# Attention scores in plain fp32 on 64 rows a head, both heads of a pair together, in a kernel whose order is planned

## The chip, the cores and the metric

The kernel runs on one core of one Trainium2 chip. The metric is the device time of one execution in microseconds (us), lower is better. A core has a matrix engine (PE in the profile, its weight loads PEld), a vector engine (DVE), an activation engine (ACT), a general engine (POOL), and queues that start transfers (SP and ACT here). Matmuls write to PSUM, a small memory of banks; the rest works in on-chip SBUF.

## The reference, cut to what matters

```python
B, H, S, D = 4, 8, 576, 64
scores = scale * q @ k.T                 # per batch and head: 576 x 64 times 64 x 576
scores += bias(pos)                      # a small network on relative positions, same for all batches
attn = exp(scores - max); attn /= sum
x = (attn @ v)                           # heads side by side: B x 576 x 512
h = gelu(x @ w_in); u, v = halves(h)     # 512 -> 1024
x = x + (u * (w_sg @ norm(v) + b_sg)) @ w_out
theta = x @ w_theta                      # second block
u = x + w_tok_r @ (x cos theta) + w_tok_i @ (x sin theta)
out = u + relu(u @ w_ch)
```

## The kernel before, in words

The program has four stretches. First the position bias of all heads is built (tiles `mk`, `pb`, `bt`, `cc`, `bias`). Then comes attention, four batches of four **pairs** of heads, with the first half of the MLP of batches 0 to 2 and the reading of its weights (`rawwi`, `cvawi`, `wi`, `ws`) woven between. Then the second half of the MLP (`op`) with the reading of the later weights (`wo`, `wt`, `wk`), and last the second block (`tp`, `yp`, `cp`).

A head has 576 query rows: four tiles of 128 (`t` = 0 to 3) and a remainder of 64. The remainders of the two heads of a pair share one tile (kind 2), so a pair has nine tiles. For each tile: the scores are made by PE into a PSUM tile `s` of two banks (two halves of 288 keys); DVE adds the bias and takes the extreme of each row (`e`, `m`); ACT takes the exponential with its row sums (`e`, `sums`), ACT copies it to 16 bits (`p`) and POOL subtracts to get the low part; a DMA transpose on SP's queue turns `p` into `pT`; PE multiplies by `v` into `px` (14 matmuls). There are two `s` tiles, so one can be filled while the other is read. At the end of a head (`group_end`) DVE divides `px` by the sums into `xf` and splits it into `x16` (shown as `x`), and after the ninth tile one DMA transpose makes `xp` of the pair, which goes to memory as `dx`.

PE takes the scores in the reduced format `float32r`. To keep precision `prep` splits, for each head, k into a high and a low part (`kh`, `kl`) and q likewise. Queries stand in `qs` with the high part on partitions 0 to 63 and the low part on 64 to 127; k is held twice, on both halves. So each score half is two matmuls over all 128 rows: `kh` and `kl` against `qs`. `prep` runs once a head: loads `raw` (k twice and v) and `rq` (q), copies `kh` and `qs`, subtractions `kl` and `qs`, and v in two 16-bit parts (`v`).

What runs in which order is decided when the program is built. Every operation is recorded; a planner (`Rec.plan`) plays through a model of the engines and always issues, per engine, the ready operation with the smallest key. The key is a due time in the code plus a number per tile name from the table `SHIFT`; where an operation may go to one of several engines, the table `BIAS` weighs the choice. Each engine then executes its list strictly in that order. All work is emitted from one line (L366 before), so the profile is read by tile names.

Of the kernel before, what the change touches and what calls it, by code (L numbers as in the profile page):

```python
# [218 lines left out]
}  # L219
SHIFT = {  # L220
    "aw": -17.4929, "bias": 41.9326, "biasr": -68.9186, "bsg": 97.9286, "bt": -5.7555, "c": -279.9533, "ca": 22.1144,
    "cc": 295.8081, "ch": -73.6056, "ci": 36.2217, "cl": 17.4554, "cp": 15.2786, "cvaw_ch": 69.6045,
    "cvaw_out": -194.7794, "cvaw_theta": 8.5825, "cvaw_tok": -207.7246, "cvawi": -0.5182, "cvsw_ch": 161.0008,
    "cvsw_out": 0.6877, "cvsw_theta": -99.9127, "cvsw_tok": 85.3798, "cvswi": 2.3671, "ds": 47.8704, "e": -0.6132,
    "eps": 169.8, "fa_c": -50.561, "fa_v": 185.4902, "fa_wi": -255.4938, "fa_ws": 58.9062, "fb_c": -277.5272,
    "fb_v": 19.4726, "fb_wi": -86.0368, "fb_ws": 64.453, "fc_c": 164.9752, "fc_v": 223.2589, "fc_wi": 7.0491,
    "fc_ws": 28.1163, "fd_c": -314.7184, "fd_v": -444.6712, "fd_wi": -6.1476, "fd_ws": -20.5742, "fs_c": 244.1602,
    "fs_v": -273.363, "fs_wi": -108.0749, "fs_ws": -26.7084, "g": 98.9891, "gg": 3.2775, "ghs": -197.3784,
    "gr": 14.9268, "gsc": -167.0231, "gts": 44.5279, "gtu": -15.6392, "gtv": -6.823, "halfpi": 90.4852, "i": 26.7498,
# [3 lines left out]
    "prow": -7.3266, "ps_wi": 22.646, "ps_ws": -28.4781, "px": -152.186, "qs": -4.2259, "r": 3.9345, "raw": -5.9457,  # L233
    "raww_ch": -200.3987, "raww_out": -60.0335, "raww_theta": 85.7967, "raww_tok": 89.0463, "rawwi": -219.9835,
# [346 lines left out]
class K:  # L581
# [257 lines left out]
    def prep(self, b, h):  # L839
        nc, a = self.nc, self.p_att  # L840
        u = f"{b}_{h}"
        qs = self.qs[(b * H + h) % 3]
        raw = a.tile([P, 2, S], F32, tag="raw", bufs=1, name=f"raw{u}")
        qr = a.tile([64, S], F32, tag="rq", bufs=1, name=f"rq{u}")
        kh = a.tile([P, S], F32R, tag="kh", bufs=3, name=f"kh{u}")
        kl = a.tile([P, S], F32R, tag="kl", bufs=3, name=f"kl{u}")
# [9 lines left out]
        self.v16[h] = v16  # L856
        self.cp(v16[:, 0], vr, self.sv)
        nc.vector.scalar_tensor_tensor(v16[:, 1, 0:5], vr[:, 0:5], self.sv, v16[:, 0, 0:5],
                                       op0=ALU.mult, op1=ALU.subtract)

    def att_tile(self, b, p, kind, t, sums, px):
        nc, a = self.nc, self.p_att
        u = f"{b}_{p}_{kind}_{t}"
        ps = self.ps_s.tile([P, 2, 512], F32, tag="sc", bufs=2, name=f"s{u}")
        hd = (self.hd[2 * p], self.hd[2 * p + 1])
        if kind < 2:
            qs, kh, kl = hd[kind]
            ops = [(qs[:, 128 + t * P:128 + (t + 1) * P], m) for m in (kh, kl)]
            bias = self.bm[t][:, 2 * p + kind]
        else:  # L870
            ops = [(hd[1][0][:, 0:128], hd[1][1]), (hd[0][0][:, 64:128], hd[0][1]),
                   (hd[0][0][:, 64:128], hd[0][2]), (hd[1][0][:, 0:128], hd[1][2])]
            bias = self.bm[4][:, p]
        for i, (w, m) in enumerate(ops):
            for n in range(2):
                nc.tensor.matmul(ps[:w.shape[1], n, :SH], w, m[:, n * SH:(n + 1) * SH],
                                 start=(i == 0), stop=(i == len(ops) - 1))
# [8 lines left out]
        self.exps.append(nc.scalar.activation(s, s, AF.Exp, bias=m[:, 1:2], scale=-1.0, accum_out=sums[:, t:t + 1]))  # L886
# [454 lines left out]
```

## Time and profile before

| | before |
|---|---|
| median of 3 runs, us | 963.27 (957.67 to 965.01) |
| span of the profiled execution, us | 948.8 |
| mean granted TensorE clock | 0.881 |
| busy: PE, DVE, ACT, POOL | 736.5, 747.9, 562.5, 441.5 us |

The span runs from the first to the last instruction. The time of the profiled execution itself is not listed apart from the three runs; their median is 14.5 us over the span, which lies before the first and behind the last instruction. Engine rows give busy time and, behind the bar, the idle time just before such instructions and what ended it. Busy PE time counts the tail of a matmul too, so a full bar is not full throughput.

### The profile page before, as it was taken

How to read it: one execution, taken by the hardware profiler on the slowest of the kernel's cores; microseconds unless marked ns; L12 is line 12 of the kernel's file. 1: busy time of each engine (PE TensorE's matmuls, PEld its weight loads, DVE VectorE, ACT ScalarE, POOL GpSimd, SP SyncE). 2: the span in 40 equal slices, each digit the busy share in tenths (PEclk: the TensorE clock that was granted, in tenths of full speed). 3: DMA queues.
4: the chain of work that ended last, by engine and by line, in shares of the span. 5: the costliest groups of instructions: out<-in, count | busy, mean ns of one | idle time of the engine just before them, and what ended most of it. 6: DMA issues, size and time to landing. Idle time of an engine off the chain costs nothing.

```text
span 948.8 us, 19542 instructions
## 1 busy us (share of the span) xinstructions
PE 736.5 (78%) x7322; PEld 598.6 (63%) x7322; DVE 747.9 (79%) x1544; ACT 562.5 (59%) x1144; POOL 441.5 (47%) x373
## 2 busy tenths in 40 slices
PE   4345445665575895979878989899778999999998
PEld 3345444554464664655555655576757899999998
DVE  8798978889987788998999796898998884372622
ACT  7413148868776777877877684765555673261510
POOL 1667784545545464564556563145643532041310
PEclk9667876756669888899979999999988999999999
DMA  7300019889899999999989995645541110010001
GB/s 250 104 1 2 1 30 255 166 167 217 152 197 207 204 194 183 192 225 218 190 186 199 231 179 154 208 138 176 182 134 48 34 52 34 1 51 1 26 26 50
DMA packets 223871, 124.79 MB, mean 132 GB/s; under 512 B 195616, under 2 KB 195744, under 8 KB 223776
## 3 DMA queue, kind: packets, MB, share of 16 engines
q1 hardware_dynamic: 214560, 101.88, 50.0%
q10 hardware_dynamic: 9216, 21.67, 7.9%
q8 instruction: 57, 0.93, 0.4%
q14 instruction: 38, 0.31, 0.1%
HBM read 62.17 MB, written 14.16 MB: 80 GB/s over the span
## 4 chain that ended last, share of the span: by engine, by line
PE 38%; DVE 28%; DMA 15%; issue 10%; ACT 7%; POOL 1%; SPq 0%; ACTq 0%; DVEq 0%; POOLq 0%
PE yp L366 11%; DMA pT<-p 6%; DVE mk L366 5%; PE cp L366 4%; PE s L366 4%; DVE e L366 4%; PE op L366 3%; PE tp L366 3%; PE pb L366 3%; PE px L366 3%; DMA xp<-x 3%; PE up L366 2%; DVE x L366 2%; DVE cvaw_tok L366 2%; PE sp L366 2%
## 5 line engine op out<-in xcount | busy, mean ns | idle before, releaser
L366 POOL TENSOR_TENSOR p<-e,p 128x576 f16<-128x576 f32 x144 | 194.4, 1358 | 152.7 <-ACT p L366 132.5
L366 PE MATMUL s<-kh,qs 128*128 128x288 f32 (+1 forms) x320 | 94.0, 390 | 63.9 <-DVE m L366 39.6
L366 ACT ACTIVATE e<-e,m 128x576 f32<-128x576 f32 x144 | 110.4, 767 | 42.1 <-DVE m L366 37.7
L366 PE MATMUL px<-v,pT 128*128 128x64 f16 (+1 forms) x2240 | 102.5, 206 | 41.1 <-DMA pT<-p 34.3
L366 PEld LDWEIGHTS <-pT 128*128 128x128 f16 (+1 forms) x2240 | 89.0, 110 | 68.8 <-DMA pT<-p 46.1
L366 PE MATMUL yp<-wk,z 128*128 128x288 f32 x864 | 118.3, 296 | 0.7 <-ACT z L366 0.4
L366 PEld LDWEIGHTS yp<-wk,z 128*128 128x128 f32 x864 | 115.6, 188 | 1.8 <-ACT z L366 0.9
L366 PEld LDWEIGHTS s<-kh,qs 128*128 128x128 f32 (+1 forms) x320 | 59.3, 222 | 85.5 <-DVE m L366 31.7
L366 PE MATMUL pb<-ch,mk 128*128 128x64 f16 x720 | 60.0, 213 | 65.6 <-ACT cc L366 34.4
L366 DVE CUSTOM_DVE_ANT_0 e<-s,bias 128x576 f32<-128x576 f32 x128 | 95.7, 751 | 13.0 <-PE s L366 11.4
L366 ACT ACTIVATE p<-e 128x576 f16<-128x576 f32 x140 | 92.8, 671 | 18.3 <-DMA pT<-p 13.5
L366 PEld LDWEIGHTS <-mk 128*128 128x128 f16 x1440 | 58.4, 111 | 68.0 <-DVE mk L366 54.8
L366 PE MATMUL s<-kl,qs 128*128 128x288 f32 (+1 forms) x320 | 84.9, 362 | 6.4 <-DVE kl L366 6.1
L366 DVE TENSOR_TENSOR mk<-ds,th 128x2048 f16<-128x2048 f16 x45 | 79.5, 1817 | 5.2 <-PE pb L366 5.1
L366 POOL TENSOR_TENSOR bias<-bt,cc 128x512 f32<-128x512 f32 x36 | 62.1, 1745 | 42.8 <-ACT cc L366 24.0
L366 PE MATMUL op<-sp_g,wo 128*128 128x288 f32 x384 | 65.0, 328 | 14.6 <-DVE x L366 9.3
L366 PEld LDWEIGHTS op<-sp_g,wo 128*128 128x128 f32 x384 | 59.1, 212 | 21.3 <-DVE x L366 7.0
L366 PEld LDWEIGHTS s<-kl,qs 128*128 128x128 f32 (+1 forms) x320 | 62.1, 228 | 10.2 <-DVE kl L366 9.2
L366 ACT ACTIVATE cc<-pb,ci 128x512 f32<-128x512 f32 x45 | 29.6, 683 | 62.5 <-DVE bt L366 56.7
L366 PE MATMUL vp<-wi,xT 128*128 128x512 f16 (+1 forms) x240 | 64.2, 395 | 2.2 <-DVE gg L366 2.2
L366 PE MATMUL sp<-ws,n 128*128 128x64 f16 (+1 forms) x384 | 58.7, 293 | 2.8 <-DVE n L366 2.7
L366 DVE TENSOR_TENSOR x<-x,yp 128x576 f32<-128x576 f32 x16 | 12.1, 754 | 61.6 <-PE yp L366 61.6
(228 smaller groups left out, 1651.5 us busy)
## 6 DMA issues: line engine op xcount, KB each, us to landing
raw<-kv ACTq DMA_DIRECT2D x19, 576.0 KB, 4.9
raw<-kv SPq DMA_DIRECT2D x13, 576.0 KB, 4.7
raww_tok<-w_tok SPq DMA_DIRECT2D x18, 288.0 KB, 3.0
vr<-v_all SPq DMA_DIRECT2D x12, 384.0 KB, 3.8
xx<-dx SPq DMA_DIRECT2D x16, 288.0 KB, 3.2
out<-oo SPq DMA_DIRECT2D x16, 288.0 KB, 2.1
xT<-dx SPq DMA_DIRECT2D x7, 576.0 KB, 5.2
gr<-dg SPq DMA_DIRECT2D x14, 288.0 KB, 3.3
```

Of the source, the lines that this page charges most:

```text
L366: getattr(getattr(self.nc, name), m)(*[res(x) for x in a], **out)
```

## The change

The two heads of a pair now lie side by side: k and q of head 0 on partitions 0 to 63, of head 1 on 64 to 127, unsplit (`kq`). A score half is one plain fp32 matmul over the 64 rows of its head; the four of a tile pair are issued in the order head 0, head 1, head 0, head 1, each head into its own `s` tile. `kh`, `kl`, `qs` and `rq` are gone. `prep` runs once a pair. The main ends of both heads are one (`pair_main`, 8 columns of sums, `xf` 128x512), and the remainder tile stands at the start of the pair (`pair_rem`), but in the first pair at its end. The planner's model of a 64-row matmul is changed, and both tables and a few of its constants have new values; some loads and weights may now choose another queue or engine.

```diff
 BIAS = {
-    ("gg", "gpsimd"): -9.3524, ("gg", "vector"): -1.4198, ("kh", "scalar"): -12.8265, ("kh", "vector"): 14.8773,
+    ("bsg", "scalar"): -41.5201, ("bsg", "sync"): -39.1168, ("g", "scalar"): -6.4798, ("g", "sync"): -12.4768,
...
-        return rhs.cols * (4.0 if rhs.t.dt == F32 else 1.068 if rhs.t.dt == F32R else 1.0), rhs.shape[0] / P
+        n = rhs.cols * (4.0 if rhs.t.dt == F32 else 1.068 if rhs.t.dt == F32R else 1.0)
+        return (n / 2 if rhs.shape[0] == 64 else n), rhs.shape[0] / P
...
-        kr, vr = raw[:, 0], raw[:, 1].rearrange("p (c d) -> p c d", d=D)
-        self.cp(kh, kr)
-        self.tt(("gpsimd", "vector"), kl, kr, kh.bitcast(F32), ALU.subtract)
-        self.cp(qs[0:64, 64:640], qr)
-        self.tt(("gpsimd", "vector"), qs[64:P, 64:640], qr, qs[0:64, 64:640].bitcast(F32), ALU.subtract)
-        v16 = a.tile([P, 2, 9, D], F16, tag="v16", bufs=3, name=f"v16{u}")
+        kq = a.tile([P, 2, S], F32, tag="kq", bufs=2, name=f"kq{u}")
+        raw = a.tile([P, 2, S], F32, tag="raw", bufs=1, name=f"raw{u}")
+        for o in (self.ld(kq, self.d["kq"][b, p]), self.ld(raw, self.d["vp"][b, p])):
+            nc.dep(o, self.th)
+        v16 = a.tile([P, 2, 2, 9, D], F16, tag="v16", bufs=2, name=f"v16{u}")
...
+    def scores(self, b, p, t):
+        k, q = self.kq[:, 0], self.kq[:, 1]
+        if t < 4:
+            tiles = [self.ps_s.tile([P, 2, 512], F32, tag="sc", bufs=2, name=f"s{b}_{p}_{e}_{t}") for e in range(2)]
+            parts = [(tiles[e], slice(0, P), slice(64 * e, 64 * e + 64)) for e in range(2)]
+        else:
+            tiles = [self.ps_s.tile([P, 2, 512], F32, tag="sc", bufs=2, name=f"s{b}_{p}_2_0")]
+            parts = [(tiles[0], slice(64 * e, 64 * e + 64), slice(64 * e, 64 * e + 64)) for e in range(2)]
+        for n in range(2):
+            for ps, o, r in parts:
+                ops.append(nc.tensor.matmul(ps[o, n, :SH], q[r, t * P:min(S, t * P + P)], k[r, n * SH:(n + 1) * SH],
+                                            start=True, stop=True))
+        for o in ops:
+            for ps in tiles:
+                nc.dep(o, ps.t.first)
...
+    def pair_main(self, b, p, sums, x16):
+        r = self.inverse(sums, u)
+        xf = a.tile([P, 4, P], F32, tag="xf", bufs=1, name=f"xf{u}")
+        nc.vector.tensor_tensor(xf.rearrange("p t (e d) -> p (t e) d", e=2), self.px.rearrange("p t e d -> p (t e) d"),
+                                r.bc(2, D), op=ALU.mult)
+        self.cp(x16[:, :4, 0], xf)
+        self.tt(("gpsimd", "vector"), x16[:, :4, 1], xf, x16[:, :4, 0], ALU.subtract)
...
-        order = [(e, t) for e in range(2) for t in range(4)] if q else [(e, t) for t in range(4) for e in range(2)]
+        if q:
+            self.pair_rem(b, p, self.px[:, 3, 1], x16)
+        for t in range(4):
+            ps = self.scores(b, p, t)
+            for e in range(2):
+                self.att_tile(b, p, e, t, ps[e], sums[:, 2 * t + e:2 * t + e + 1], self.px[:, t, e])
+        self.pair_main(b, p, sums, x16)
```

PE's list before, in batch 2, second pair (`s2_1_0_1` is batch 2, pair 1, head 0, tile 1; `up` and `sp` are the MLP of batch 0):

```order
5591 L366 MATMUL sp0_0_5411<-ws_2204,n16_0_3909 128x512
5592 L366 LDWEIGHTS wi_2205
5593 L366 MATMUL up0_2_5412<-xT0_3904,wi_2205 128x512
5594 L366 MATMUL s2_1_0_0_5451<-kh2_2_5016,qs0_121 128x288 x2
5595 L366 MATMUL s2_1_0_1_5471<-kh2_2_5016,qs0_121 128x288 x2
5596 L366 LDWEIGHTS wi_2205
5597 L366 MATMUL up0_2_5412<-xT0_3904,wi_2205 128x512
```

An `s` row here stands for both key halves of one tile (x2); the `kl` part of both tiles follows some 30 rows further on. The same place in PE's list now:

```order
5721 L377 MATMUL px_2127<-v162_0_4647,pT2_0_1_1_5070 128x64
5722 L377 MATMUL s2_1_0_1_5168<-kq2_1_4702 128x288
5723 L377 MATMUL s2_1_1_1_5194<-kq2_1_4702 128x288
5724 L377 MATMUL s2_1_0_1_5168<-kq2_1_4702 128x288
5725 L377 MATMUL s2_1_1_1_5194<-kq2_1_4702 128x288
5726 L377 LDWEIGHTS n16_0_3950
5727 L377 MATMUL sp0_2_5028<-ws_2151,n16_0_3950 128x512
```

Before, two tiles of one head stand in the two `s` buffers, each begun with `kh` and finished with `kl` further on; now tile 1 of both heads fills both buffers in one group of four.

DVE's list before, around the first tile of that pair (`v16`, `kl`, `qs` are the preparation of pairs to come, `r` and `xf` the end of pair 0):

```order
655 L366 TENSOR_SCALAR v162_2_5345<-raw2_2_5360,fc_v_157 128x576
656 L366 TENSOR_TENSOR kl2_2_5046<-raw2_2_5360,kh2_2_5016 128x576
657 L366 SCALAR_TENSOR_TENSOR v162_2_5345<-raw2_2_5360,fc_v_157,v162_2_5345 128x320
658 L366 TENSOR_TENSOR qs1_120<-rq2_3_5214,qs1_120 64x576
659 L366 TENSOR_SCALAR r2_0_0_5355<-sm2_0_0_4780 128x4
660 L366 TENSOR_SCALAR r2_0_1_5384<-sm2_0_1_5103 128x4
661 L366 ISA e2_1_0_0_5462,m2_1_0_0_5400<-s2_1_0_0_5451,bias0_78 128x576
```

Four of these seven rows prepare heads of pairs to come. DVE's list now, around the second tile of that pair:

```order
587 L377 SCALAR_TENSOR_TENSOR gg0_2_5192<-sp0_2_5028,gsc_118,bsg_164 128x512
588 L377 TENSOR_TENSOR x16_2_0_5163<-xfr2_0_2_4888,x16_2_0_5163 64x128
589 L377 ISA e2_1_0_1_5227,m2_1_0_1_5141<-s2_1_0_1_5168,bias1_77 128x576
590 L377 ISA m2_1_0_1_5141 128x1
591 L377 TENSOR_SCALAR m2_1_0_1_5141<-m2_1_0_1_5141 128x1
592 L377 ISA e2_1_1_1_5274,m2_1_1_1_5165<-s2_1_1_1_5194,bias1_77 128x576
```

The `kl` and `qs` rows between the `e` rows are gone from DVE's list, and the `e` of head 0 and of head 1 of one tile number follow each other.

## Rows read from the trace of the kernel before

**Rows 1.** By stretch: length, busy PE, PEld, DVE, ACT, POOL, clock, DMA share, GB/s

```profile
0.00:131.00 131.00, 60.69 (x1422) 58.30 (x1423) 112.96 (x129) 50.62 (x91) 79.22 (x54) 0.79 0.20 65
131.00:300.00 169.00, 102.34 (x1020) 83.96 (x1016) 147.55 (x390) 127.31 (x298) 87.15 (x80) 0.68 0.91 184
300.00:425.00 125.00, 95.30 (x1042) 68.50 (x1041) 106.70 (x261) 94.55 (x193) 69.53 (x59) 0.87 1.01 198
425.00:583.00 158.00, 138.64 (x1515) 90.46 (x1514) 140.90 (x359) 120.10 (x239) 86.34 (x75) 0.97 0.98 192
583.00:734.00 151.00, 131.44 (x885) 98.03 (x883) 126.22 (x242) 86.17 (x180) 64.37 (x66) 0.94 0.50 155
734.00:949.00 215.00, 208.06 (x1453) 199.38 (x1451) 113.61 (x165) 83.77 (x147) 54.86 (x43) 1.00 0.09 30
```

**Rows 2.** Chain that ended last, attention only (131:583): shares by engine and tile

```profile
by line: DMA pT<-p 13.6%; PE s L366 9.1%; issue 8.7%; DVE e L366 7.9%; PE px L366 5.8%; DMA xp<-x 5.3%; DMA rawwi<-w_in 3.6%; DVE x L366 3.4%; DMA raw<-kv 3.3%; DVE cvawi L366 2.8%; PE vp L366 2.5%; ACT e L366 2.5%; DVE kl L366 2.4%; DVE gt
```

**Rows 3.** The same chain piece by piece, from 400:425 (start, us, what)

```profile
412.92 1.72 DVE qs L366
...
419.07 0.58 ACT kh L366
...
419.68 1.89 DVE kl L366
...
421.61 0.52 PE s L366 x2
```

**Rows 4.** Instructions of tiles kl, qs, x, xp: ns min/median/max

```profile
L366 DVE TENSOR_TENSOR kl<-raw,kh x32: 726/755/1876, 32.9 to 550.8; 128x576 fp32r<-128x576 f32 x32
L366 DVE TENSOR_TENSOR qs<-rq,qs x30: 743/752/1800, 24.5 to 535.5; 64x576 fp32r<-64x576 f32 x30
L366 DVE TENSOR_TENSOR x<-xf,x x32: 408/418/1515, 177.9 to 577.0; 128x256 f16<-128x256 f32 x32
L366 DVE TENSOR_TENSOR rk<-xp,rk x18: 676/692/694, 704.3 to 902.5; 128x512 f32<-128x512 f32 x16, 64x512 f32<-64x512 f32 x2
```

**Rows 5.** Groups by tile and shape: busy us, mean ns, idle before and its releasers

```profile
L366 DVE TENSOR_TENSOR qs<-rq,qs 64x576 fp32r<-64x576 f32 x30 | 29.4, 979 | 5.0 <-ACT qs L366 2.7 <-DMA raw<-kv 1.4
L366 DVE TENSOR_TENSOR kl<-raw,kh 128x576 fp32r<-128x576 f32 x32 | 29.2, 913 | 4.6 <-ACT kh L366 4.5
L366 ACT ACTIVATE kh<-raw 128x576 fp32r<-128x576 f32 x32 | 21.5, 673 | 9.7 <-DMA raw<-kv 7.9 <-DMA xp<-x 1.5
L366 ACT ACTIVATE qs<-rq 64x576 fp32r<-64x576 f32 x29 | 19.6, 678 | 9.4 <-DMA rq<-qt 4.2 <-PE s L366 4.2 <-issue 0.3
L366 DVE CUSTOM_DVE_ANT_0 e<-s,bias 128x576 f32<-128x576 f32 x128 | 95.7, 751 | 13.0 <-PE s L366 11.4 <-POOL p L366 0.4
L366 PE MATMUL s<-kh,qs 128*128 128x288 f32 x288 | 88.6, 397 | 63.9 <-DVE m L366 39.6 <-ACT kh L366 21.2 <-DVE gts L366 1.5
L366 PE MATMUL s<-kl,qs 128*128 128x288 f32 x288 | 79.5, 366 | 6.4 <-DVE kl L366 6.1
L366 POOL TENSOR_TENSOR wk<-wr_w_tok,wk 128x576 fp32r<-128x576 f32 x9 | 13.8, 1532 | 9.3 <-ACT wk L366 9.3
```

**Rows 6.** Single matmuls, ns min/median/max: scores, plain fp32, fp32 transposes

```profile
L366 PE MATMUL s<-kl,qs x320: 288/297/610, 131.9 to 563.2; 128*128 128x288 f32 x144, 128*64 128x288 f32 x16
L366 PE MATMUL pbv<-ssv,ones x2: 251/262/272, 132.8 to 132.9; 128*128 128x2 f32 x2
L366 PE MATMUL xp<-ident,x x64: 270/273/329, 677.8 to 891.3; 128*128 128x128 f32 x64
```

**Rows 7.** Matmuls in order of time (start, us), three places at full clock

```profile
484.50 0.29 PE L366 MATMUL s<-kl,qs 128*64 128x288 f32 x1
...
484.64 0.58 PE L366 MATMUL px<-v,pT 128*128 128x64 f16 x14
...
544.75 0.29 PE L366 MATMUL s<-kh,qs 128*128 128x288 f32 x1
544.88 0.42 PE L366 MATMUL s<-kl,qs 128*128 128x288 f32 x2
```

More of the change, by code (lines that the diff above doesn't have):

```diff
@@ L223 @@
[L223 to L227, printed above, removed]
@@ L857, in prep @@
         self.cp(v16[:, 0], vr, self.sv)
-        nc.vector.scalar_tensor_tensor(v16[:, 1, 0:5], vr[:, 0:5], self.sv, v16[:, 0, 0:5],
+        nc.vector.scalar_tensor_tensor(v16[:, 1, :, 0:5], vr[:, :, 0:5], self.sv, v16[:, 0, :, 0:5],
                                        op0=ALU.mult, op1=ALU.subtract)
-    def att_tile(self, b, p, kind, t, sums, px):
+        self.kq, self.v16 = kq, v16
+    def scores(self, b, p, t):
+        nc = self.nc
+        k, q = self.kq[:, 0], self.kq[:, 1]
+        ops, tiles = [], []
+        if t < 4:
[11 more added lines that the diff above has]
+                nc.dep(o, ps.t.first)
+        return tiles
@@ L862, in att_tile @@
+    def att_tile(self, b, p, kind, t, ps, sums, px):
         nc, a = self.nc, self.p_att
         u = f"{b}_{p}_{kind}_{t}"
[L864 to L877, printed above, removed]
+        bias = self.bm[t][:, 2 * p + kind] if kind < 2 else self.bm[4][:, p]
         s = a.tile([P, S], F32, tag="s", bufs=4, name=f"e{u}")
@@ L885, in att_tile @@
                     ("gpsimd", "tensor_tensor", (m[:, 1:2], m[:, 0:1], self.ln2e), {"op": ALU.add}))
-        self.exps.append(nc.scalar.activation(s, s, AF.Exp, bias=m[:, 1:2], scale=-1.0, accum_out=sums[:, t:t + 1]))
+        self.exps.append(nc.scalar.activation(s, s, AF.Exp, bias=m[:, 1:2], scale=-1.0, accum_out=sums))
         p16 = a.tile([P, 2, S], F16, tag="p16", bufs=4, name=f"p{u}")
@@ L891, in att_tile @@
         nc.sync.dma_start_transpose(out=pT, in_=p16.rearrange("p s j -> p (s j)"))
+        v = self.v16
         if kind < 2:
-            outs = [(px[:, t], slice(0, P), self.v16[2 * p + kind])]
+            outs = [(px, slice(0, P), kind)]
         else:
-            outs = [(px[0:64, 0], slice(0, 64), self.v16[2 * p]),
-                    (px[64:P, 0], slice(64, P), self.v16[2 * p + 1])]
-        for o, cs, v in outs:
+            outs = [(px[64 * e:64 * e + 64], slice(64 * e, 64 * e + 64), e) for e in range(2)]
@@ L898, in att_tile @@
+        for o, cs, e in outs:
             seq = [(c, 0) for c in range(9)] + [(c, 1) for c in range(5)]
             for c, i in seq:
-                nc.tensor.matmul(o, pT[:, c, cs], v[:, i, c], start=(c == 0 and i == 0), stop=(c == 4 and i == 1))
-    def group_end(self, b, p, kind, sums, px, x16, xp):
-        nc, a = self.nc, self.p_att
-        u = f"{b}_{p}_{kind}"
-        n = 4 if kind < 2 else 1
-        r = a.tile([P, 4], F32, tag="r", bufs=2, name=f"r{u}")
-        nc.vector.tensor_scalar(r[:, :n], sums[:, :n], 1e-9 * ESC, None, op0=ALU.add)
-        nc.vector.reciprocal(r[:, :n], r[:, :n])
-        if kind < 2:
-            xf = a.tile([P, 4, D], F32, tag="xf", bufs=1, name=f"xf{u}")
-            nc.vector.tensor_tensor(xf, px, r[:, :4].bc(2, D), op=ALU.mult)
-            ks = slice(kind * D, (kind + 1) * D)
-            self.cp(x16[:, :4, 0, ks], xf)
-            self.tt(("gpsimd", "vector"), x16[:, :4, 1, ks], xf, x16[:, :4, 0, ks], ALU.subtract)
-        else:
-            xf = a.tile([64, P], F32, tag="xfr", name=f"xfr{u}")
-            nc.vector.tensor_scalar(xf[:, 0:64], px[0:64, 0], r[0:64, 0:1], None, op0=ALU.mult)
-            nc.vector.tensor_scalar(xf[:, 64:P], px[64:P, 0], r[64:P, 0:1], None, op0=ALU.mult)
-            self.cp(x16[0:64, 4, 0], xf)
-            self.tt(("vector", "gpsimd"), x16[64:P, 4, 0], xf, x16[0:64, 4, 0], ALU.subtract)
@@ new lines, in att_tile, with inverse, pair_rem @@
+                nc.tensor.matmul(o, pT[:, c, cs], v[:, i, e, c], start=(c == 0 and i == 0), stop=(c == 4 and i == 1))
+    def inverse(self, sums, u):
+        nc = self.nc
+        n = sums.shape[1]
+        r = self.p_att.tile([P, n], F32, tag=f"r{n}", bufs=2, name=f"r{u}")
+        nc.vector.tensor_scalar(r, sums, 1e-9 * ESC, None, op0=ALU.add)
+        nc.vector.reciprocal(r, r)
+        return r
+    def pair_rem(self, b, p, px, x16):
+        nc, a = self.nc, self.p_att
+        u = f"{b}_{p}_2"
+        sums = a.tile([P, 1], F32, tag="sumr", bufs=2, name=f"sr_{u}")
+        self.att_tile(b, p, 2, 0, self.scores(b, p, 4)[0], sums, px)
+        r = self.inverse(sums, u)
+        xf = a.tile([64, P], F32, tag="xfr", name=f"xfr{u}")
+        nc.vector.tensor_scalar(xf[:, 0:64], px[0:64], r[0:64], None, op0=ALU.mult)
+        nc.vector.tensor_scalar(xf[:, 64:P], px[64:P], r[64:P], None, op0=ALU.mult)
+        self.cp(x16[0:64, 4, 0], xf)
+        self.tt(("vector", "gpsimd"), x16[64:P, 4, 0], xf, x16[0:64, 4, 0], ALU.subtract)
@@ new lines, in pair_main @@
+    def pair_main(self, b, p, sums, x16):
+        nc, a = self.nc, self.p_att
+        u = f"{b}_{p}"
+        r = self.inverse(sums, u)
+        xf = a.tile([P, 4, P], F32, tag="xf", bufs=1, name=f"xf{u}")
[3 more added lines that the diff above has]
+        self.tt(("gpsimd", "vector"), x16[:, :4, 1], xf, x16[:, :4, 0], ALU.subtract)
@@ L925, in att_pair @@
         k0 = 9 * q
-        for e in range(2):
-            nc.key = T0 + TS * (k0 - 8 + 4 * e)
-            self.prep(b, 2 * p + e)
+        nc.key = T0 + TS * (k0 - 8)
+        self.prep(b, p)
         x16 = a.tile([P, 5, 2, P], F16, tag="x16", name=f"x16_{b}_{p}")
         xp = a.tile([P, 2 * S], F16, tag="xp", bufs=1, name=f"xp{b}_{p}")
-        grp = [(a.tile([P, 4], F32, tag="sums", bufs=4, name=f"sm{b}_{p}_{e}"),
-                self.px[:, e]) for e in range(2)]
-        order = [(e, t) for e in range(2) for t in range(4)] if q else [(e, t) for t in range(4) for e in range(2)]
-        left = [4, 4]
-        for i, (e, t) in enumerate(order):
-            nc.key = T0 + TS * (k0 + i)
-            self.att_tile(b, p, e, t, *grp[e])
-            left[e] -= 1
-            if left[e] == 0:
-                self.group_end(b, p, e, *grp[e], x16, xp)
-        nc.key = T0 + TS * (k0 + 8)
-        g = (a.tile([P, 4], F32, tag="sums", bufs=4, name=f"sm{b}_{p}_2"),
-             self.px[:, 0, 3:4])
-        self.att_tile(b, p, 2, 0, *g)
-        self.group_end(b, p, 2, *g, x16, xp)
+        sums = a.tile([P, 8], F32, tag="sums", bufs=2, name=f"sm{b}_{p}")
+        nc.key = T0 + TS * k0
+        if q:
+            self.pair_rem(b, p, self.px[:, 3, 1], x16)
+        for t in range(4):
+            nc.key = T0 + TS * (k0 + 2 * t + (q > 0))
+            ps = self.scores(b, p, t)
+            for e in range(2):
+                nc.key = T0 + TS * (k0 + 2 * t + e + (q > 0))
+                self.att_tile(b, p, e, t, ps[e], sums[:, 2 * t + e:2 * t + e + 1], self.px[:, t, e])
+        self.pair_main(b, p, sums, x16)
+        if not q:
+            nc.key = T0 + TS * (k0 + 8)
+            self.pair_rem(b, p, self.px[:, 0, 0], x16)
         nc.sync.dma_start_transpose(out=xp.rearrange("p (t k) -> p t k", k=P),
@@ L1230, in build @@
         self.ps_x = nc.pool("psx", "left", PSUM)
-        self.px = self.ps_x.tile([P, 2, 4, D], F32, name="px")
+        self.px = self.ps_x.tile([P, 4, 2, D], F32, name="px")
         self.ps_c = nc.pool("psc", "left", PSUM)
```

76 lines of the change are left out of this document (40 added, 36 removed), and 34 rows, old and new, of tables (BIAS, SHIFT).

## The prediction

> **What bounds the kernel now.** I first cut the run into stretches [rows 1]. The change touches attention, 131 to 583 us: 452 of 949 us. There DVE is the busiest engine in each of the three stretches (147.5 of 169, 106.7 of 125, 140.9 of 158 us): 395 us, 87%. ACT has 342 us, PE 336 (with the tails of its matmuls, and at a granted clock of 0.68, 0.87 and 0.97), POOL 243. The DMA share stands at 0.91 to 1.01, but it sums the packet times of several queues, so it may count waiting. The last stretch, 734 to 949, is PE's (208 of 215 us at full clock) and has nothing that the change alters.
>
> Then I read the chain of waits for attention alone [rows 2]. It is not one engine: DMA transposes `pT` 13.6% (61 us), PE's scores 9.1% (41 us), DVE's `e` 7.9% (36 us), issue 8.7%, `kl` 2.4% (11 us). Piece by piece it shows how preparation gets in [rows 3]: within nine microseconds of one pair `qs` 1.72, `kh` 0.58 and `kl` 1.89 us lie on it, and behind `kl` the scores. These are the instructions that go. Third, the groups with their waits [rows 5]: PE idles 63.9 us before scores with `kh`, of that 39.6 until DVE has read a score buffer (`m`) and 21.2 until ACT has made `kh`; 6.1 more for `kl`. DVE waits 11.4 us for scores before `e`.
>
> **Preparation removed.** 32 `kl` at a median of 0.755 us and 30 `qs` at 0.752 [rows 4] are 24.2 + 22.6 = 46.8 us of DVE. As busy time the two groups count 29.2 + 29.4 = 58.6 [rows 5]; single ones take up to 1.9 us [rows 4], so some 12 us is waiting inside them that other DVE instructions may inherit. ACT loses 32 `kh` and 29 `qs`: 21.5 + 19.6 = 41 us [rows 5]. Their loads go as well, 32 x 144 KB, and k is no longer loaded twice; what this gives on the DMA engines I count at nothing.
>
> **Ends merged.** Per pair five DVE operations become one for both heads (low part of v, `xf`, low part of `x`, sums plus a constant, reciprocal). Two of 256 elements take 2 x 0.418, one of 512 takes 0.692 [rows 4], so a merge saves about 0.144 us; 5 x 16 x 0.144 = 11.5 us. Together DVE sheds 58 us (medians) to 70 (busy), say 64 of 395.
>
> **What that is worth.** The least is what the chain shows: `kl` 11 us, `qs` about as much (as many instructions of the same length), `kh` some 3: 25 us. The most is DVE staying 87% busy with 64 us less: 64 / 0.87 = 73 us. I take 60, near the upper end, since DVE leads in all three stretches and PE's 27 us of waiting for `kh` and `kl` go too. It is not the whole, because ACT (342 - 41 = 301 us) and DVE (331) then come close to each other, and the transposes stay on the chain.
>
> **Scores in fp32.** A tile pair had eight score matmuls of 288 columns, which at full clock start 0.13 us apart (544.75 to 544.88 [rows 7]): 1.04 us. Now it has four in plain fp32. The trace has plain fp32 only with 2 columns; the one matmul in the code appears there as two [rows 6]. An fp32 transpose of 128 columns lasts at least 270 ns, a score matmul 288 [rows 6] of which 130 is its pitch and 158 its tail; so 128 fp32 columns cost 112 ns, 0.875 ns each against 0.45. Two passes over 288 columns at that rate are 0.50 us. Four of them one after the other are 2.0 us; if the two heads overlap perfectly and a column costs only 0.45, four are 0.52 us. That is the range. If each matmul may start as soon as the one before it has started and its own half of the rows is free, the order head 0, head 1 makes the second pass of one overlap the first pass of the next: five passes in place of eight, 1.26 us. I take that. Over 80 groups (64 pairs of tiles, 16 remainders) it is (1.26 - 1.04) x 80 = 18 us more of PE. PE is not the busiest engine, so I put 10 on the path.
>
> What the trace shows of matmuls beside each other is only that they follow at their pitch. The Trainium skill, "TensorE: Matmul & The Clock Gate", section "Part 3: Packing small matmuls — row/col tiling", states that matmuls on different row groups run concurrently, starting about 4 ns apart. No run here shows it; the serial case is the second rival.
>
> **Both buffers at once.** The four matmuls are issued together and need both `s` buffers; before, each tile took one. So DVE's second `e` of a tile pair must be over before PE can finish the next pair, and behind the waiting matmul stand `px` and the MLP, and then DVE's next `e`. At worst that exposes one `e` per pair, 64 x 0.751 [rows 5] = 48 us; at best nothing, where DVE has other work between the pairs. The list shows such work, `gtu` and `gg`, between most of them. I take 5 us.
>
> **One `xf` per pair.** `px` of both heads is read by one instruction of about 0.69 us, and the first `px` of the next pair, now that of the remainder, must wait for it. The moved remainder brings its scores, exponential, split, its `pT` transpose on SP ahead of the eight others, and its `px`; in return `xp` no longer waits for it at the end. From 0 to 16 x 0.69 = 11 us; I take 3, since PE has MLP matmuls to put between.
>
> **Elsewhere.** The tables are new. The nine low parts of `wk`, on POOL at 1.532 us [rows 5], all go to DVE, at `kl`'s 0.755 some 7 us, in a stretch where DVE is busy 126 of 151 us [rows 1] and POOL 64. Either could win 7 us; I take 0.
>
> **Sum.** 60 - 10 - 5 - 3 = 42 us. The profiled span becomes 948.8 - 42 = 907; the 14.5 us between the span and the median of the runs stay, so 963.3 - 42 = 921.
>
> **Rivals.** First, *DVE's relief carries over whole* and the new waits vanish in the order: 963 - 73 = 890. For it: DVE's lead in every stretch. Against it: the chain, with 61 us of transposes. Chance 0.1.
>
> Second, *the halves don't overlap*, the slower side. Then a group costs 2.0 us, 0.96 more than before, 77 us over 80 groups at full clock. Since a group holds both `s` buffers, DVE's next `e` waits for it, so all of it can fall on the path: 963 - 60 + 8 + 77 = 988. The point from which it decides is a group of 1.04 + 52 / 80 = 1.7 us: above it the change loses. A granted clock at half, which attention's first stretch shows for much of its time (0.68 [rows 1]), makes the 1.26 us into 2.5 and works in the same direction. Chance 0.1.
>
> Third, *the transposes and loads set the pace*: attention then gains only the 25 us that the chain shows, less the 18 of new costs: 956. For it speaks the DMA share near 1 and `pT` at the head of the chain; against it that DVE is idle for only 13%. Chance 0.12.
>
> Fourth, *the array is emptied at each change between whole rows and half rows*. A group is entered and left, so 160 times, and each time the tail of a matmul, 0.158 us, is exposed: 25 us of PE; all on the path, 921 + 25 = 946. The trace has one change of shape, of the columns: `s` at 128*64 starts at 484.50 and `px` at 128*128 follows 0.14 us later [rows 7], so no emptying there. It has no change of rows. The Trainium skill, "TensorEngine Tiling (Array Packing)", section "Tiling Modes", says that a change of tiling mode drains the engine; it speaks against this change, the column case in the trace does not agree, and the row case no run here shows. Chance 0.08.
>
> **How the numbers follow.** My own case has 0.6. Its unknown costs alone reach from 963 - 70 to 963 - 10. The range of 887 to 962 takes in the first, third and fourth rival and leaves out the second. About 1% is what a measurement of this kernel can tell from no change. Faster by more: my case nearly whole (0.58), first (0.1), fourth (0.08), a little of the third: 0.77. Within it: most of the third and a rest, 0.12. Slower: 0.11.
>
> **What would show it.** Right: attention ends near 540 in place of 583, DVE's busy time there falls by 58 to 70 us, score groups at full clock last about 1.3 us and start as pairs. Serial halves show as groups of 2 us, or a new large wait of `e` for `s`. Emptying shows as gaps before and after each group. If transposes bound it, DVE's busy time falls but its share too, with `px` waiting longer for `pT`. What would make me wrong beyond this: a granted clock in attention that is lower than the 0.68 to 0.97 of before [rows 1]; or a new order that costs time in bias or MLP, which no row of before can tell.

## The result, and the profile after

| | before | after | after, run again |
|---|---|---|---|
| median, us | 963.09 (957.67 to 965.01) | 920.50 (909.19 to 925.51) | 916.07 (899.22 to 925.41) |
| ratio to before, 95% interval | | 0.9536 (0.946 to 0.9611) | 0.9452 (0.9372 to 0.9533) |
| span of the profiled execution, us | 948.8 | 920.2 | 907.5 |

Forecast were 921 us and a range of 887 to 962. The ratios leave out executions more than 1.5% above the quickest of the same kernel, four of six in the second measurement of after, so they need not be the quotient of the medians; with all its executions that measurement gives 0.955. The same kernel measured twice differs by 8 us in its ratio: a variant of it is told apart only where its interval lies beyond both of these. Where two costs are given below, the one against the first ratio, 0.9536, is the firmer.

One figure ahead of the prediction was wrong. The profiled execution of after took 922.0 us with a span of 920.2: 1.8 us lie outside the span, not 14.5. The profiled execution of before was a quick one (948.8 + 1.8 = 950.6, under all four runs of the table). So the profiles show 28.6 us of difference where the medians show 43.

Page of after, part 1, busy time of each engine:

```profile
PE 742.5 (81%) x7322; PEld 558.2 (61%) x7322; DVE 660.5 (72%) x1391; ACT 525.5 (57%) x1064; POOL 421.0 (46%) x363
```

DVE lost 87 us (747.9 to 660.5), ACT 37; PE stayed. By stretch as in [rows 1], of after: length, busy PE, PEld, DVE, ACT, POOL, clock, DMA share, GB/s.

```profile
0.00:126.00 126.00, 62.20 (x1442) 59.62 (x1442) 109.80 (x127) 48.19 (x85) 82.67 (x56) 0.81 0.21 72
126.00:290.00 164.00, 113.29 (x1094) 72.24 (x1095) 124.82 (x352) 125.10 (x293) 93.21 (x87) 0.74 0.99 203
290.00:410.00 120.00, 102.20 (x1116) 58.98 (x1114) 82.00 (x220) 82.72 (x163) 64.95 (x61) 0.91 0.99 182
410.00:555.00 145.00, 125.97 (x1335) 71.03 (x1332) 101.49 (x268) 99.08 (x198) 76.97 (x71) 0.91 0.93 178
555.00:702.00 147.00, 130.25 (x892) 96.97 (x890) 130.91 (x262) 89.47 (x186) 52.82 (x52) 0.95 0.52 161
702.00:920.00 218.00, 208.55 (x1453) 199.38 (x1451) 111.51 (x165) 81.01 (x143) 50.38 (x40) 1.00 0.08 29
```

For a sharper cut I take attention from the last matmul of the bias to the start of the last transpose of `xp`. The same view over that stage, of before, of after, and of after run again:

```profile
131.60:580.00 448.40, 332.71 (x3540) 241.13 (x3537) 392.21 (x1004) 340.55 (x726) 241.75 (x211) 0.83 0.97 192
```

```profile
126.00:552.00 426.00, 338.46 (x3526) 200.89 (x3527) 307.00 (x836) 305.58 (x651) 235.12 (x217) 0.84 0.97 189
```

```profile
127.00:538.50 411.50, 331.13 (x3538) 196.74 (x3535) 307.78 (x836) 305.49 (x651) 234.35 (x216) 0.87 1.00 196
```

DVE does 85 us less in attention, yet the stage is only 22 us shorter (37 in the second run): DVE's share falls from 87% to 72% (75%). `kl` and `qs` took 57 of the 85 us. The five merged operations, of `r`, `x`, `xf` and `v`, shrank by 27, and `r` alone by 12: its addition took 508 ns a half before, most of it a wait inside a few of them (the median, with the remainders, was 160), and takes 241 for both halves now. The 22 us and 6 more in the bias make up the 28.6 of the profiles; behind attention all three take 368 to 369.

The groups of after that answer to [rows 5] (busy us, mean ns, idle before and releasers):

```profile
L377 PE MATMUL s<-kq 64*128 64x288 f32 (+1 forms) x640 | 138.1, 508 | 15.9 <-DVE m L377 10.1
L377 DVE CUSTOM_DVE_ANT_0 e<-s,bias 128x576 f32<-128x576 f32 x128 | 95.7, 752 | 62.6 <-PE s L377 47.6
L377 PE MATMUL px<-v,pT 128*128 128x64 f16 (+1 forms) x2240 | 100.3, 204 | 64.8 <-DMA pT<-p 55.2
L377 ACT ACTIVATE p<-e 128x576 f16<-128x576 f32 x142 | 94.1, 671 | 40.2 <-DMA pT<-p 38.0
```

The waiting has turned round. PE idled 39.6 us for score buffers that DVE was still reading (`m`) and 21.2 for `kh`; that is 10.1 now. In its place DVE waits 47.6 us for scores where it waited 11.4, PE waits 55.2 for `pT`, where the waits of before say 34.3 for the same stage, and ACT 38.0 where they say 13.5:

```profile
PE s L366 <- DVE m L366: 39.6, 28, 4.4
PE px L366 <- DMA pT<-p: 34.3, 23, 7.1
...
ACT p L366 <- DMA pT<-p: 13.5, 10, 4.7
```

In DVE's three longest waits for scores, 20 us in all, the scores stand in PE's list behind a `px` that waits for its transpose. The order of time in after shows one (start, us, engine, what, idle before and releaser): `px` and ACT's `p` resume at 330.9 as a transpose lands, the scores follow, and DVE's `e` has waited 7.2 us for them.

```profile
330.92 0.93 PE L377 MATMUL px<-v,pT 128*128 128x64 f16 x14 [4.57 <-DMA pT<-p]
330.95 0.68 ACT L377 ACTIVATE p<-e 128x576 f16<-128x576 f32 x1 [4.79 <-DMA pT<-p]
...
332.63 2.29 PE L377 MATMUL s<-kq 64*128 64x288 f32 x8
...
335.06 0.76 DVE L377 CUSTOM_DVE_ANT_0 e<-s,bias 128x576 f32<-128x576 f32 x1 [7.21 <-PE s L377]
```

The group takes 2.29 us there: PE had stood idle for 4.57 us, and the granted clock of 330:335 is 0.51, about the lower of its two levels (1.2 and 2.4 GHz). For the rest of DVE's waits for scores, 29 of 48 us, PE is at work on its list and not waiting for `pT`.

A score group at full rate, with the MLP matmul ahead of it (the first row is of the window 470.725 to 470.735):

```profile
470.42 0.38 PE L377 MATMUL up<-xT,wi 128*128 128x512 f16 x1
...
470.73 1.24 PE L377 MATMUL s<-kq 64*128 64x288 f32 x8
...
471.90 1.25 PE L377 MATMUL up<-xT,wi 128*128 128x512 f16 x5
```

Four matmuls of the code are eight records, and the next matmul starts 1.17 us after the first: 1.26 was forecast. Narrow windows of the same stretch show how they start: two by 470.745, four by 471.09.

```profile
470.73 0.51 PE L377 MATMUL s<-kq 64*128 64x288 f32 x2
...
470.73 0.76 PE L377 MATMUL s<-kq 64*128 64x288 f32 x4
```

In the single records of the trace the pairs start at 470.731, 471.078, 471.320 and 471.563, the two of a pair 7 ns apart: the heads overlap. A step is 0.243 us for 288 columns, 0.84 ns a column (0.875 was estimated).

### The profile page after: what moved, and what is told of

The parts are those of the page before. It is cut to its first block, busy times and chain, and to the rows that moved or that the text cites. A ratio compares the mean times of both kernels' runs of the same rounds, so it can differ in the third digit from the quotient of the medians.

```text
span 920.2 us, 19119 instructions
## 1 busy us (share of the span) xinstructions
PE 742.5 (81%) x7322; PEld 558.2 (61%) x7322; DVE 660.5 (72%) x1391; ACT 525.5 (57%) x1064; POOL 421.0 (46%) x363
## 5 line engine op out<-in xcount | busy, mean ns | idle before, releaser
L377 POOL TENSOR_TENSOR p<-e,p 128x576 f16<-128x576 f32 x144 | 189.1, 1322 | 127.7 <-ACT p L377 84.2
L377 PEld LDWEIGHTS <-pT 128*128 128x128 f16 (+1 forms) x2240 | 87.1, 108 | 114.3 <-DMA pT<-p 66.5
L377 PE MATMUL px<-v,pT 128*128 128x64 f16 (+1 forms) x2240 | 100.3, 204 | 64.8 <-DMA pT<-p 55.2
L377 PE MATMUL s<-kq 64*128 64x288 f32 (+1 forms) x640 | 138.1, 508 | 15.9 <-DVE m L377 10.1
L377 DVE CUSTOM_DVE_ANT_0 e<-s,bias 128x576 f32<-128x576 f32 x128 | 95.7, 752 | 62.6 <-PE s L377 47.6
L377 PEld LDWEIGHTS s<-kq 64*128 64x128 f32 (+1 forms) x640 | 71.4, 212 | 54.4 <-DVE m L377 22.1
L377 POOL TENSOR_TENSOR bias<-bt,cc 128x512 f32<-128x512 f32 x36 | 63.6, 1789 | 34.3 <-ACT cc L377 34.3
L377 PE MATMUL op<-sp_g,wo 128*128 128x288 f32 x384 | 61.9, 320 | 14.1 <-DVE x L377 12.8
L377 PEld LDWEIGHTS op<-sp_g,wo 128*128 128x128 f32 x384 | 57.2, 206 | 19.0 <-issue 10.6
L377 PE MATMUL pb<-cl,mk 128*128 128x64 f16 x720 | 60.7, 214 | 0.0
L377 PE MATMUL up<-xT,wi 128*128 128x64 f16 (+1 forms) x384 | 57.8, 297 | 0.0
```

What stands on the lines that cost most here:

```text
L377: getattr(getattr(self.nc, name), m)(*[res(x) for x in a], **out)
```

## The experiments

All orders are those of the kernel they start from, instruction for instruction, except where the text says "planned anew". "Ratio" is to before, with its interval.

**Do the halves overlap only because the heads alternate?** `a_serial` changes the order inside each group of four, in the built list, to head 0, head 0, head 1, head 1.

```diff
+            for k, o in zip(pos, (g[0], g[2], g[1], g[3])):
+                order[k] = (o, 0)
```

> The changed kernel in its own order, but within each group of four score matmuls head 0, head 0, head 1, head 1 in place of head 0, head 1, head 0, head 1. If the halves overlap because heads alternate, a group of 1.24 us at full clock becomes seven passes of 0.24 us, 1.7 us, 35 us of PE in all over 80 groups, of which some half falls on the path: 938 us. If the engine pairs them by itself, or the overlap is worth nothing to the whole: 920 us.

Measured: 912.59 us, ratio 0.951 (0.9465 to 0.9555): no change. The order of time shows a group of the same length, and a narrow window at its start shows two records begun at once (the second row is of the window 443.83 to 443.85):

```profile
443.83 1.25 PE L378 MATMUL s<-kq 64*128 64x288 f32 x8
...
443.83 0.52 PE L378 MATMUL s<-kq 64*128 64x288 f32 x2
```

Head by head, seven or eight steps of 0.243 us would be 1.7 to 1.94 us. So the halves overlap in this order too. The records don't name the head, and the two of a pair might be the two records of one matmul. The trace speaks against that: it keeps which records raise a semaphore, and a tile does so in the last record of its last matmul. Of 44 groups of two tiles whose eight records lie close together, 31 raise both in the last pair, so the pair holds one record of each head; only four raise them in the fourth and eighth record, as the order of the list would have it. So PE mostly starts head 1's matmul ahead of head 0's second: that each engine executes its list strictly in order, as the text ahead of the prediction has it, does not hold for these halves.

**What is DVE's and ACT's relief worth?** `b_noprep` is before without the subtractions `kl` and `qs` (the second matmul reads `kh` again, the low half of q is zeros; low parts are left out of the scores).

```diff
-        self.tt(("gpsimd", "vector"), kl, kr, kh.bitcast(F32), ALU.subtract)
+        self.tt(("gpsimd", "vector"), kl, kr, kh.bitcast(F32), ALU.subtract).skip = True
-        self.tt(("gpsimd", "vector"), qs[64:P, 64:640], qr, qs[0:64, 64:640].bitcast(F32), ALU.subtract)
+        self.tt(("gpsimd", "vector"), qs[64:P, 64:640], qr, qs[0:64, 64:640].bitcast(F32), ALU.subtract).skip = True
```

> The kernel before in its own order, without the 32 kl and 32 qs low-part subtractions on DVE and POOL (the scores use kh in place of kl and zeros for the low part of q, so the low parts are left out of the computation): the same 47 to 59 us of DVE away, kh, the high part of qs, the loads and the eight matmuls a pair of tiles stay. If DVE's relief is worth nearly its length: 963 - 45 = 918 us. If other waits take its place: 963 - 20 = 943 us.

Measured: 940.18 us, 0.9864 (0.9813 to 0.9914), 13 us faster (8 to 18). The zeros are 27 small ACT copies at the start; the bias ends 2 us later. Its attention, in the view by stage, and the chain of waits of 126 to 540 us:

```profile
133.50:568.00 434.50, 328.96 (x3537) 241.02 (x3533) 339.25 (x943) 338.70 (x724) 231.64 (x207) 0.83 1.00 198
```

```profile
by line: DMA pT<-p 25.6%; issue 8.3%; DVE e L366 6.5%; PE s L366 5.7%; PE px L366 4.2%; POOL p L366 4.0%; DMA raw<-kv 3.6%; ACT p L366 3.1%; DVE x L366 3.0%; DMA rawwi<-w_in 2.8%; ACT e L366 2.8%; DVE cvawi L366 1.9%; DMA rs<-w_sg 1.9%; DVE
```

DVE does 53 us less and the stage is 14 shorter. In the chain [rows 2] `pT` stood at 13.6% (11.7% in 126 to 540); it is 25.6% now, so on the chain the transposes take what DVE gives up. The engines' own waits rose less: PE's for `pT` from 34.3 to 41.4 us, DVE's for scores from 13.6 to 22.4.

From the other side, `a_dve64` adds a DVE subtraction of 128x576 to a spare tile ahead of `e` of head 0, 64 of them; `a_act64` adds 64 copies of 128x576 on ACT behind the exponential of head 0; `a_both64` has both.

```diff
+            o.extra = lambda: nc.nc.vector.tensor_tensor(self.junk.real(), self.bm[0][:, 0].real(), self.bm[0][:, 1].real(), op=ALU.subtract)
...
+            self.exps[-1].extra = lambda: nc.nc.scalar.activation(self.junk.real(), self.bm[0][:, 0].real(), AF.Copy)
```

> The changed kernel in its own order, with 64 added DVE subtractions of 128x576 (one ahead of the e of head 0 of each tile), as long as the kl and qs that the change removed: 64 x 0.755 = 48 us of DVE given back, nothing else. If DVE's relief is what made the gain and DVE still sets the pace, most of it comes back: 920 + 45 = 965 us. If the pace is now set by the transposes and by PE's list waiting for them, DVE has room and it costs some 15: 935 us.

> The changed kernel in its own order, with 64 added ACT copies of 128x576 (one ahead of the copy p of head 0 of each tile), as many and as long as the kh and qs that the change removed: 64 x 0.67 = 43 us of ACT given back. If ACT's relief was a main part of the gain: 950 us. If ACT has as much room as DVE showed: 930 us.

> The changed kernel in its own order with both additions at once, 64 DVE subtractions (48 us) and 64 ACT copies (43 us). If the two reliefs are independent, the sum of the single costs, 13 + 0: 931 us. If each alone is hidden only because the other engine has room, so that the removed preparation counts as a whole: 960 us.

Measured: `a_dve64` 924.23 us, 0.9672 (0.9621 to 0.9724); `a_act64` 912.0, 0.951 (0.9466 to 0.9555); `a_both64` 920.87, 0.962 (0.9566 to 0.9673). Against the two ratios of after, 48 us of DVE cost 13 to 21, 43 us of ACT nothing that shows, and both together no more than DVE's alone (the interval of `a_both64` touches that of after's first measurement). Attention in `a_dve64`, and its wait of DVE for scores, which was 48.5 in the same view of after:

```profile
126.00:559.00 433.00, 345.24 (x3539) 206.18 (x3536) 365.65 (x902) 307.07 (x651) 244.86 (x218) 0.84 0.95 186
```

```profile
DVE e L377 <- PE s L377: 21.4, 12, 7.9
```

The new wait of `e` for `s` is partly slack: it shrinks by 27 us (17 against the second profile's 38.4) as DVE gets 48 us (59 as busy time) more to do. Of DVE's time 27 to 44% reach the end here, and 25% in `b_noprep` (13 of 53).

**Does PE's score time count?** `b_nokl` is `b_noprep` also without the second score matmul of each half in full tiles, 256 instructions, 33 us of PE at the pitch of 0.13 [rows 7].

```diff
+                if kind < 2 and i:
+                    o.skip = True
```

> The kernel before in its own order without kl and the low part of q, as in the second run, and also without the second matmul of every score half of the 128 main tiles (256 score matmuls of 288 columns less, 33 us of PE at full clock; the low parts are left out of the computation). If PE's time for scores is on the path: 20 us less than without kl alone, 925 us. If PE only waits elsewhere instead: 943 us.

Measured: 943.52 us, 0.9881 (0.9817 to 0.9944), against 0.9864 with them: nothing. In attention:

```profile
133.00:568.50 435.50, 302.96 (x3280) 208.77 (x3278) 334.02 (x944) 335.97 (x725) 230.78 (x207) 0.77 1.02 197
```

PE's busy time fell by 26 us, the stage is no shorter, and the granted clock is 0.77 in place of 0.83: what was left ran slower.

**What are the merges worth?** `a_unmerge` is after with the five merged operations of a pair issued as two halves again, in the place of the merged one: 80 more instructions.

```diff
+        nc.halves(o, lambda e: ("tensor_tensor", (xf[:, 2 * e:2 * e + 2].rearrange("p t (e d) -> p (t e) d", e=2),
+                                                  self.px[:, 2 * e:2 * e + 2].rearrange("p t e d -> p (t e) d"),
+                                                  r[:, 4 * e:4 * e + 4].bc(2, D)), dict(op=ALU.mult)))
```

> The changed kernel in its own order, with the five merged DVE operations of a pair (low part of v, sums plus a constant, reciprocal, xf, low part of x) issued as two halves each: 80 more instructions, 11.5 us of DVE. If DVE has as much room as the 64 additions showed (13 us for 48): 3 us or less, 920 us. If the end of a pair is on the path: 10 us or more, 930 us.

Measured: 926.98 us, 0.9698 (0.9646 to 0.975): 16 to 24 us slower than after. The instructions of `xf` and `x` (ns min/median/max), of after and of `a_unmerge`:

```profile
L377 DVE TENSOR_TENSOR xf<-px,r x16: 677/684/692, 167.6 to 549.4; 128x512 f32<-128x512 f32 x16
L377 DVE TENSOR_TENSOR x<-xf,x x16: 672/690/1707, 174.2 to 550.9; 128x512 f16<-128x512 f32 x16
```

```profile
L377 DVE TENSOR_TENSOR xf<-px,r x32: 406/414/425, 172.4 to 551.1; 128x256 f32<-128x256 f32 x32
L377 DVE TENSOR_TENSOR x<-xf,x x32: 405/419/1459, 178.7 to 552.6; 128x256 f16<-128x256 f32 x32
```

A merge of `xf` saves 2 x 414 - 684 = 144 ns, as forecast. By stage (attention alone) DVE has 7 to 8 us more than in the two profiles of after:

```profile
126.00:553.00 427.00, 336.16 (x3553) 201.81 (x3550) 314.83 (x918) 306.81 (x652) 234.87 (x218) 0.85 0.97 189
```

Its profile, 924.9 us of span, stands 5 and 17 over those of after; 3 of it lie behind attention (372 against 369). Why so little DVE time costs 16 to 24 is not settled; that the end of a pair stands between its last `px` and its `xp`, with little beside it, fits but was only argued.

**What did the new tables give?** `a_oldtab` is after with the tables and constants of before, planned anew by these. They were not made for its tiles (`kq` has no entry).

```diff
-    ("bsg", "scalar"): -41.5201, ("bsg", "sync"): -39.1168, ("g", "scalar"): -6.4798, ("g", "sync"): -12.4768,
+    ("gg", "gpsimd"): -9.3524, ("gg", "vector"): -1.4198, ("kh", "scalar"): -12.8265, ("kh", "vector"): 14.8773,
...
```

> The changed kernel with both tables and the planner's constants of the kernel before (names that are new get no number), so all of the edit but the refitted order. If the refit gives a large part of the gain: 945 us. If the removed work gives it by itself: 925 us.

Measured: 942.56 us, 0.9824 (0.9772 to 0.9875): 17 us faster than before, 28 to 36 slower than after. By stage (attention; second half of the MLP; second block), and the chain of waits of 126 to 540 us:

```profile
132.00:563.00 431.00, 360.61 (x3557) 205.09 (x3554) 321.02 (x866) 301.39 (x638) 236.49 (x208) 0.85 0.96 188
563.00:725.00 162.00, 128.29 (x857) 95.29 (x855) 123.40 (x247) 87.91 (x185) 68.00 (x68) 0.91 0.49 149
725.00:943.00 218.00, 212.11 (x1474) 202.50 (x1473) 109.87 (x160) 82.30 (x143) 51.40 (x40) 1.00 0.08 27
```

```profile
by line: DMA pT<-p 21.5%; PE s L366 16.6%; PE px L366 10.3%; issue 8.7%; PE vp L366 6.3%; POOL p L366 4.4%; PE sp L366 4.0%; DVE e L366 3.9%; PE up L366 3.5%; DMA xp<-x 2.2%; DVE x L366 1.9%; ACT e L366 1.7%; DVE v L366 1.5%; ACT p L366 1.4
```

Against the stages of after (126, 426, 149, 219 us) the old tables lose 6 in the bias, 5 in attention and 13 in the second half of the MLP; against the second profile 5, 20 and, behind attention, 12. So between 46 and 79% of what the refit gave lies outside the stage whose arithmetic was changed. DVE's `e` has left the chain's head (3.9%, from 7.9), and `pT` and scores lead it.

**Do the transposes set the pace?** `a_t5` and `b_t5` transpose five of a tile's nine blocks, and `px` reads those five again for the others (so the transposes of the other four blocks are left out).

```diff
-        nc.sync.dma_start_transpose(out=pT, in_=p16.rearrange("p s j -> p (s j)"))
+        nc.sync.dma_start_transpose(out=pT[:, 0:5], in_=p16.rearrange("p s j -> p (s j)")[:, 0:640])
-                nc.tensor.matmul(o, pT[:, c, cs], v[:, i, e, c], start=(c == 0 and i == 0), stop=(c == 4 and i == 1))
+                nc.tensor.matmul(o, pT[:, c % 5, cs], v[:, i, e, c], start=(c == 0 and i == 0), stop=(c == 4 and i == 1))
```

> The changed kernel in its own order, with the pT transposes cut to 5 of their 9 blocks of 128 (px reads the first five blocks twice; four blocks of the transposed probabilities are left out of the computation). If the transposes set the pace of attention now: some 40 us less, 880 us. If DVE or the order of the lists sets it: 10 us or less, 910 us or more.

> The kernel before in its own order, with the pT transposes cut to 5 of their 9 blocks in the same way (four blocks of the transposed probabilities are left out of the computation). If DVE led in the kernel before, the transposes cost it little: 963 - 10 = 953 us. If they already set the pace there: 963 - 35 = 928 us, and the change could not take that away.

Measured: `a_t5` 894.01 us, 0.9349 (0.929 to 0.9408), 10 to 18 us faster than after (its interval touches that of the second measurement); `b_t5` 942.67, 0.9871 (0.9817 to 0.9926), 12 faster than before (7 to 18). Transposes that set the pace were expected to give 35 to 40 us: they are one limit beside others, in both kernels. That they count for more after the change than before is not shown. Attention of `a_t5`, and PE's wait for `pT` (55.2 in after):

```profile
128.00:522.00 394.00, 329.25 (x3534) 197.72 (x3532) 305.88 (x836) 303.87 (x650) 234.36 (x216) 0.86 0.74 157
```

```profile
PE px L377 <- DMA pT<-p: 28.0, 15, 4.5
```

The other way, `a_buf6` gives the tiles `p` and `pT` six buffers in place of four, planned anew.

```diff
-        p16 = a.tile([P, 2, S], F16, tag="p16", bufs=4, name=f"p{u}")
+        p16 = a.tile([P, 2, S], F16, tag="p16", bufs=6, name=f"p{u}")
-        pT = a.tile([P, 9, P], F16, tag="pT", bufs=4, name=f"pT{u}")
+        pT = a.tile([P, 9, P], F16, tag="pT", bufs=6, name=f"pT{u}")
```

> The changed kernel with six buffers each for p16 and pT in place of four; the planner makes a new order with the same tables. ACT waits 38 us for pT before p, and PE 55 us. If the waits come from too few buffers: 905 us. If the transposes themselves are the limit, buffers only queue more of them: 920 us, give or take 10 for an order that isn't refitted.

Measured: 928.95 us, 0.9714 (0.9655 to 0.9772): 17 to 25 slower. By stage:

```profile
128.00:533.00 405.00, 332.51 (x3492) 198.48 (x3490) 303.46 (x820) 298.96 (x639) 234.81 (x208) 0.85 1.01 199
533.00:709.00 176.00, 144.02 (x948) 101.83 (x946) 152.25 (x312) 107.53 (x225) 60.16 (x64) 0.91 0.47 144
```

Attention is the shortest with full transposes, 405 us against 426 and 411, and the stage behind it 27 longer (176 against 149): DVE does 152 us there in place of 131. Work was pushed out of attention; that tables fitted to six buffers would place it better was not tried.

**After itself, once more.**

> The changed kernel once more, as it is, beside the three others on the same chip: 0.954 of the kernel before within 0.008, since its single runs lay between 907 and 926 us.

Measured: 916.07 us, as in the first table.

## Why the prediction was right, and where it was not

The time was right to 1 us by luck: two terms of the sum were far off in opposite directions and met.

**Relief of DVE and ACT, "I take 60".** This step was mis-sized. DVE shed 85 us of attention's busy time, more than the 58 to 70; but the preparation, put back or taken away alone, is worth 13 us (`b_noprep`, 53 us of DVE) and a like load costs 13 to 21 (`a_dve64`); ACT's 41 us are worth nothing (`a_act64`). DVE led in every stretch by its busy share, and I took the share for the bound. The third rival was nearer in the mechanism: its sign, a lower share of DVE with `px` waiting longer for `pT`, is what the profiles show, and 25 us was all that the chain of before showed. But it has transposes set the pace, and with four ninths of them away the gain is 10 to 18 us. The merges went the other way: counted at 11.5 us of DVE, they cost 16 to 24 to undo, and why is open.

**Elsewhere, 0 with 7 us to either side.** This step failed. The tables are worth 28 to 36 us to the new program, by `a_oldtab`. Without them the change gave 17 us, 946 on the scale of the forecast: the sum of the other terms, 42, was 25 too high in that order, which tables made for other tiles gave. What a refit of the tables would have given to the kernel before was not tried, so how much of the 28 to 36 belongs to the change stays open. The parts don't add up either: 17 with old tables against 13 for the preparation alone leaves little for merges that are worth 16 to 24 in the new order.

**Scores in fp32, 1.26 us a group, 10 us on the path.** The length was right (1.24, and 1.17 to the next matmul), though not as five passes: four paired steps of 0.243 us, and 0.1 us each in the first step and on leaving; 0.09 ahead of the group makes it 1.26. Of the 18 us more of PE its busy time in attention shows 6 (332.7 to 338.5), and none in the second profile. Nor would they have lain on the path, as far as the kernel before tells: 33 us of scores taken away there gave nothing (`b_nokl`).

**Halves that don't overlap (988)** fell, by the single records and by `a_serial`. The Trainium skill, "TensorE: Matmul & The Clock Gate", "Part 3: Packing small matmuls — row/col tiling", gives a start about 4 ns apart for different row groups; here it is 7 ns, and the concurrency is as it says. The same section says that matmuls start strictly in program order; the length of `a_serial` and its semaphores do not agree with it for halves of the rows.

**Emptying at each change of rows (946)** is real, and the time of PE that it was given, 25 us, is about right; that it adds to the forecast is not. In the group at 470.73 the MLP matmul ahead starts 0.309 us earlier, where at full clock one such follows another after 0.216 (median): 0.09 us before the group. Its first step is 0.347 us in place of 0.243: 0.1 us more; emptying and the first load of weights can't be told apart there. Its last stream, begun at 471.563, ends by the step of 0.243 at 471.806, and the next matmul starts at 471.904: 0.1 us at exit. Together 80 x 0.29 = 23 us of PE, and they stand within the 1.26 us, because four steps took less than the five passes. The Trainium skill, "TensorEngine Tiling (Array Packing)", "Tiling Modes", has the drain without a price; the trace agrees that there is one.

The prediction also read the trace of before wrongly: `s` at 128*64 is not its only change of columns. The 128*64 matmuls of the fp16 tiles `vp` and `px` have the gap too (three windows of before: 455.5 to 455.6, 455.85 to 455.9, 456.05 to 456.2):

```profile
455.40 0.39 PE L366 MATMUL vp<-wi,xT 128*128 128x512 f16 x1
...
455.63 0.38 PE L366 MATMUL vp<-wi,xT 128*128 128x512 f16 x1
...
455.94 0.40 PE L366 MATMUL vp<-wi,xT 128*64 128x512 f16 x1
```

The first two start 0.23 us apart (0.216 at the median of such pairs), the last two, with the change, 0.31. So the size of the gap, 0.09 us, could be read before the change; why `s` at 128*64 has none is open.

**Both buffers at once, 5 us; one `xf`, 3 us.** PE's wait for buffers fell (39.6 to 10.1), which fits the two `e` that it depends on standing one behind the other in DVE's list. DVE's wait for scores grew (11.4 to 47.6), and `a_dve64` could use 17 to 27 us of it; what the rest costs the whole no run isolates. PE's waits for `xf` and `xfr` in after are

```profile
PE px L377 <- DVE xf L377: 4.7, 3, 3.2
PE px L377 <- DVE xfr L377: 4.5, 4, 2.4
```

together 9.2 us, against 4.9 for the same tiles before: the 3 us was of the right order.

**What would show it.** Attention was to end near 540 in place of 583, where the last `dx` is issued: by that mark it ended at 555 and, in the second profile, 542. The clock did not fall (0.83 to 0.84 and 0.87).

## What to carry to other kernels

A busy share of 87% is not a bound: take away or add a known amount on that engine, in the same order, before its time is priced; here 25 to 44% of it reached the end. Where a planner's tables are refitted with a change, price the refit as a term of its own, and look for it in the stages that the change does not touch. A total that comes out right proves no term of its sum: here terms of 42 us that gave 17 met a missing one of 28 to 36.

## What the runs showed of the hardware

- Plain fp32 matmuls of 288 columns run as two records of 0.243 us each, 0.84 ns a column, and those of different halves of the rows run side by side, started 7 ns apart (13 ns in `a_serial`), whichever of the two orders the list has. Listed head by head, head 1's first matmul mostly starts ahead of head 0's second.
- With 256 matmuls taken out of attention the granted clock there was 0.77 in place of 0.83, and PE's busy time 26 us less. After an idle wait of 4.57 us a score group took 2.29 us, at a granted clock of 0.51, where one at full clock takes 1.24.
- A group over half the rows among matmuls over all rows has a gap of 0.09 us ahead of it and 0.1 us behind it, and a first step longer by 0.1 us. The gap ahead stands at the same 0.09 us where fp16 matmuls change from 128 to 64 columns, and not where `s` does.
